# Two transformer layers on one core: the first five attention units of layer 2 take their keys in two parts

## The chip, the cores and the metric

The kernel runs on one core of a Trainium2 chip. Five engines work side by side and meet only through semaphores: TensorE (PE, matrix products into PSUM), VectorE (DVE), ScalarE (ACT), GpSimd (POOL) and SyncE (SP, which here issues the DMAs). The metric is the device time of one execution in microseconds (us). Before the change the median of three runs is 2412.53 us (2412.13 to 2412.62).

## The reference

Two layers, each an attention block and a gated feed-forward block, both with a layer norm ahead and a residual around them. The sequence has 2048 tokens of width 512, the attention 32 heads of 16, the feed-forward a width of 1792. Both layers use the same weights.

```python
def _A_ref(x, wqkv, wo):
    ...
    scores = jnp.einsum("bhqd,bhkd->bhqk", q, k) * (Dh ** -0.5)
    p = _softmax(scores, axis=-1)
    o = jnp.einsum("bhqk,bhkd->bhqd", p, v)
    return (...o...) @ wo

def _B_ref(x, w_gate, w_up, w_down):
    return (_gelu(x @ w_gate) * (x @ w_up)) @ w_down

x = A_x
x = x + _A_ref(_layernorm(x), A_wqkv, A_wo)
x = x + _B_ref(_layernorm(x), B_w_gate, B_w_up, B_w_down)
x = x + _A_ref(_layernorm(x), A_wqkv, A_wo)
x = x + _B_ref(_layernorm(x), B_w_gate, B_w_up, B_w_down)
```

## The kernel before

Everything stays in on-chip memory. The attention is cut into **units**: four heads (a group `g`, of eight) times one block of queries (512, at the end of a layer less). A unit runs through two passes over all 2048 keys:

- **Pass 1** finds the maximum of each row of scores. PE multiplies 128 queries by 512 keys into one PSUM bank (L2935), DVE reduces the bank to one column of `PM` (L2950), one bank at a time ("128x1") or two banks in one instruction ("128x2"). A unit has 64 such tiles. Six small POOL operations (`fin_step`, from L1956) join the four key blocks' maxima into minus the row maximum, which is turned around (a DMA, or for the units at a layer's edge a DVE transpose into `MT`, L1972) and written by DMA into spare rows of the query tile `QT`.
- **Pass 2** multiplies in the other direction, keys by queries (L2813). The spare rows make the product come out as score minus maximum. ACT takes the exponential into one of ten slots `PT` of the buffer `SCR` (L2785), again one bank (512 columns) or two (1024) in one instruction. PE multiplies that by the values `VP`, which carry a column of ones for the row sums, and sums over all keys in PSUM bank 7 (L2838). At a unit's end `nrm` copies bank 7 to `ACCS` (ACT, L2034), and POOL divides by the row sums into `ATT`.

A **fold** takes work from DVE to ACT: PE multiplies the queries by the difference of two key blocks (`KD`), ACT writes its positive part to a slot (Relu, L2765), and one DVE instruction (L2945) adds that to the other block's scores and takes the maximum, in place of two reductions.

Beside the two passes run the projections, the output product, the layer norms and the feed-forward. Their PSUM banks are emptied by ACT or DVE. `evac` (L1592 for DVE, L1594 for ACT) and `x_add` (L2053 for DVE, L2058 for ACT) decide this by how far pass 1 is ahead of pass 2. The keys of a layer-2 block need the finished tokens of layer 1, so the keys 1536 to 2047 of layer 2 come only after the last feed-forward block of layer 1. The last block's gate uses the Gelu table of ACT, during which no exponential of pass 2 is emitted (`gel["on"]`).

The order of all instructions is made ahead of time, by a planner in the program (from L2980 on): it keeps a clock for each engine with estimated durations and emits, at each step, a pass-1 tile, a pass-2 tile or a piece of other work. A table `PLAN` gives it 20 parameters for every two pairs of pass-1 tiles (priorities, lags between the passes, how many banks each pass may take). The chip then runs the order as it stands.

At the edge between the layers the planner has this: pass 1 of the first six units of layer 2 (`n_pre=6`) does its first three key blocks as soon as these keys exist, 48 tiles for each unit, and its fourth block later. Pass 2 of a unit begins when the maximum over all four blocks is in `QT`, thus after the last keys of layer 2.

Of the kernel before, what the change touches and what calls it, by code (L numbers as in the profile page):

```python
# [12 lines left out]
AP = bass.AP  # L13

DH = 16
# [8 lines left out]
    1: (0.1, 0.0, 0.65, 0.52, 0.2, -0.3, 2, 0, 22, 16, 8, 20, 0.7, 4.0, -20, 10, 2, 2, 11, 84),  # L24
    2: (0.3, 0.25, 0.8, 0.42, 0.2, 0.0, 1, 1, 30, 92, 3, 80, 0.5, 2.5, 10, 18, 2, 1, 7, 30),
    3: (0.3, 0.5, 0.55, 0.42, 0.0, 0.0, 3, 1, 62, 92, 3, 80, 0.4, 0.5, -5, 18, 2, 4, 3, 68),
    4: (0.15, 0.25, 0.25, 0.42, 0.0, -0.2, 2, 1, 70, 160, 8, 80, 0.5, 3.0, -5, 18, 2, 3, 7, 60),
    5: (0.3, 0.25, 0.65, 0.42, 0.1, -0.05, 3, 1, 14, 92, 8, 60, 0.5, 2.5, 0, -6, 3, 3, 7, 16),
    6: (0.2, 0.0, 0.55, 0.52, 0.2, -0.05, 2, 2, 14, 44, 8, 60, 0.7, 4.0, 0, -6, 2, 1, 7, 100),
    7: (0.1, 0.05, 0.65, 0.52, 0.2, -0.05, 2, 2, 46, 160, -10, 60, 1.0, 1.5, 20, -14, 2, 2, 7, 84),  # L30
    9: (0.1, 0.05, 0.65, 0.52, 0.2, -0.05, 2, 2, 46, 160, -10, 60, 1.0, 2.5, 20, -14, 3, 2, 7, 84),
    10: (0.3, 0.05, 0.65, 0.52, 0.2, -0.05, 2, 2, 62, 68, 8, 100, 1.0, 2.0, 20, 2, 2, 2, 11, 84),
    11: (0.3, 0.25, 0.65, 0.22, 0.0, -0.05, 2, 1, 110, 124, 8, 80, 0.3, 2.5, 0, 10, 1, 3, 3, 124),
    12: (0.3, 0.25, 0.25, 0.62, 0.0, -0.05, 2, 1, 110, 124, 8, 80, 0.3, 1.0, 0, 10, 1, 3, 3, 68),
    13: (0.3, 0.25, 0.55, 0.42, 0.7, 0.0, 2, 1, 62, 92, 3, 80, 0.4, 1.5, 0, 18, 2, 1, 8, 100),
    15: (0.0, 0.05, 0.65, 0.52, 0.2, -0.05, 2, 2, 62, 68, 8, 100, 1.0, 2.0, 20, 2, 2, 2, 11, 84),
    16: (0.3, 0.35, 0.55, 0.52, 0.0, 0.0, 3, 2, 110, 100, 3, 40, 0.4, 4.0, -10, 18, 1, 4, 6, 44),
    17: (0.3, 0.25, 0.55, 0.42, 0.7, 0.0, 2, 1, 62, 92, 3, 80, 0.4, 1.5, 0, 18, 2, 1, 8, 100),
    18: (0.3, 0.35, 0.55, 0.52, 0.0, 0.0, 3, 2, 110, 100, 3, 40, 0.4, 4.0, -10, -14, 1, 4, 14, 92),
    19: (0.3, 0.05, 0.65, 0.52, 0.2, -0.05, 2, 2, 62, 68, 8, 40, 1.0, 2.0, 20, 2, 2, 2, 11, 84),  # L40
    22: (0.3, 0.25, 0.45, 0.42, 0.7, 0.0, 3, 1, 62, 92, 3, 80, 0.4, 4.0, -5, 18, 4, 1, 3, 30),
    23: (0.3, 0.05, 0.55, 0.42, 0.0, 0.0, 3, 1, 62, 92, 3, 80, 0.4, 0.5, -5, 18, 2, 4, 3, 68),
    24: (0.3, 0.05, 0.55, 0.42, 0.0, 0.0, 3, 1, 62, 92, -10, 80, 0.4, 0.5, -5, 18, 2, 4, 3, 68),
    25: (0.3, 0.05, 0.65, 0.22, 0.0, 0.0, 2, 1, 110, 124, 13, 80, 0.3, 2.5, 0, 10, 1, 3, 3, 124),
    26: (0.3, 0.25, 0.25, 0.12, 0.3, 0.0, 3, 1, 62, 92, 3, 60, 0.4, 4.0, -5, 18, 2, 1, 8, 68),
    27: (0.3, 0.25, 0.55, 0.42, 0.7, 0.0, 3, 2, 62, 92, 13, 100, 0.5, 4.0, -5, -6, 1, 3, 7, 68),
    28: (0.3, 0.25, 0.55, 0.42, 0.7, 0.0, 3, 2, 62, 92, 8, 100, 0.5, 4.0, -5, 2, 1, 3, 7, 68),
# [12 lines left out]
    41: (0.2, 0.25, 0.65, 0.62, 0.0, -0.05, 2, 0, 0, 84, 13, 40, 0.0, 0.5, -20, -14, 2, 3, 8, 92),  # L60
    43: (0.3, 0.5, 0.55, 0.52, 0.3, -0.05, 2, 0, 22, 84, 8, 20, 0.3, 2.0, 10, -14, 2, 2, 7, 84),
    45: (0.3, 0.5, 0.55, 0.52, 0.3, -0.05, 2, 0, 22, 84, 13, 20, 0.3, 2.0, 10, -14, 2, 2, 7, 84),
    47: (0.3, 0.15, 0.55, 0.82, 0.5, -0.05, 2, 2, 22, 16, 8, 60, 1.0, 0.5, -10, 10, 2, 3, 6, 84),
    48: (0.3, 0.15, 0.35, 0.32, 0.5, -0.05, 2, 2, 22, 16, 8, 60, 1.0, 0.5, 5, 10, 2, 3, 6, 84),
    49: (0.3, 0.35, 0.65, 0.82, 0.7, -0.05, 2, 0, 22, 100, 13, 40, 0.3, 2.5, -10, -14, 4, 2, 3, 0),
    50: (0.2, 0.25, 0.45, 0.62, 0.2, -0.2, 2, 2, 30, 84, 8, 60, 0.7, 4.0, 0, -6, 1, 1, 8, 100),
    51: (0.2, 0.25, 0.8, 0.62, 0.2, -0.2, 2, 2, 30, 84, 13, 60, 0.7, 4.0, 0, -6, 1, 1, 8, 100),
    52: (0.2, 0.25, 0.65, 0.62, 0.2, -0.2, 2, 2, 30, 84, 8, 60, 0.7, 4.0, 0, -6, 1, 1, 8, 100),
    53: (0.2, 0.0, 0.55, 0.32, 0.5, -0.1, 2, 0, 38, 84, 3, 100, 0.1, 2.0, 0, 6, 1, 1, 7, 60),
    54: (0.15, 0.5, 0.55, 0.82, 0.3, -0.05, 3, 2, 22, 30, 8, 60, 0.7, 2.5, 0, -14, 2, 4, 3, 100),  # L70
    55: (0.3, 0.25, 0.55, 0.42, 0.1, -0.05, 2, 1, 14, 92, 8, 60, 0.5, 2.0, 0, 18, 3, 3, 7, 44),
# [24 lines left out]
    85: (0.1, 0.35, 0.65, 0.62, 0.2, -0.3, 2, 0, 22, 16, 8, 20, 0.7, 4.0, -20, -6, 2, 3, 7, 84),
# [3109 lines left out]
```

## Time and profile before

| | |
|---|---|
| median of 3 runs | 2412.53 us |
| the profiled execution's own time | 2412.13 us |
| its span, first to last instruction | 2410.4 us |
| TensorE clock granted, mean | 0.999 |
| busy: PE, DVE, ACT, POOL | 2352.4, 2360.6, 2313.4, 1344.2 us |
| pass 1: reductions of one bank, of two | 1436, 1109 |
| pass 2: exponentials of one bank, of two | 1044, 1526 |

An execution's own time is 1.7 us longer than its span. Busy time counts an instruction from its start to its end, and what two instructions of one engine share is counted once. Fillers: the 1724 matmuls of L2968 multiply zeros to keep PE occupied, so PE's busy share says little of its real load.

### The profile page before, as it was taken

How to read it: one execution, taken by the hardware profiler on the slowest of the kernel's cores; microseconds unless marked ns; L12 is line 12 of the kernel's file. 1: busy time of each engine (PE TensorE's matmuls, PEld its weight loads, DVE VectorE, ACT ScalarE, POOL GpSimd, SP SyncE). 2: the span in 40 equal slices, each digit the busy share in tenths (PEclk: the TensorE clock that was granted, in tenths of full speed). 3: DMA queues.
4: the chain of work that ended last, by engine and by line, in shares of the span. 5: the costliest groups of instructions: out<-in, count | busy, mean ns of one | idle time of the engine just before them, and what ended most of it. 6: DMA issues, size and time to landing. Idle time of an engine off the chain costs nothing.

```text
span 2410.4 us, 69140 instructions
## 1 busy us (share of the span) xinstructions
PE 2352.4 (98%) x29692; PEld 1136.4 (47%) x29692; DVE 2360.6 (98%) x3191; ACT 2313.4 (96%) x3252; POOL 1344.2 (56%) x2239
## 2 busy tenths in 40 slices
PE   9999999999999999999999999999999999999999
PEld 4444444444444444444534555544444444444456
DVE  9999999999999999999999999999999999999994
ACT  7999999999999999999975999999999999999996
POOL 5121147967779575977742221178717882379452
PEclk9999999999999999999999999999999999999999
DMA  3110000000000001001010000000000000000000
GB/s 97 50 62 10 3 16 14 3 5 9 21 12 3 5 13 21 8 5 26 17 25 15 7 5 5 14 14 2 5 12 21 8 3 10 16 15 5 14 13 13
DMA packets 77166, 37.50 MB, mean 16 GB/s; under 512 B 59068, under 2 KB 75836, under 8 KB 76860
## 3 DMA queue, kind: packets, MB, share of 16 engines
q1 hardware_dynamic: 76860, 33.10, 5.7%
q8 instruction: 232, 3.80, 0.6%
q14 instruction: 74, 0.61, 0.1%
HBM read 9.70 MB, written 2.10 MB: 5 GB/s over the span
## 4 chain that ended last, share of the span: by engine, by line
DVE 51%; PE 32%; ACT 16%; issue 1%; POOL 0%; POOLq 0%; DVEq 0%; ACTq 0%
DVE PM L2950 46%; ACT SCR L2785 14%; PE PS L2935 11%; PE PS L1577 9%; PE PS L2838 8%; PE PS L2813 3%; DVE SCR L2945 2%; PE PS L2968 1%; ACT SCR L2765 1%; DVE HT L1375 0%; DVE ST L1629 0%; ACT SCR L2197 0%; PE PS L2758 0%; ACT HT L1594 0%; ACT SG L1594 0%
## 5 line engine op out<-in xcount | busy, mean ns | idle before, releaser
L2950 DVE TENSOR_REDUCE PM<-PS 128x1 f32<-128x512 f32 (+1 forms) x2545 | 2152.4, 916 | 9.2 <-PE PS L2935 2.5
L2785 ACT ACTIVATE SCR<-PS 128x1024 bf16<-128x1024 f32 (+1 forms) x2570 | 2012.6, 898 | 25.5 <-PE PS L2813 15.7
L2935 PE MATMUL PS<-KT,QT 32*128 32x512 bf16 x3875 | 1045.7, 385 | 41.3 <-DVE PM L2950 24.6
L2813 PE MATMUL PS<-QT,KT 32*128 32x512 bf16 (+2 forms) x5120 | 931.0, 340 | 2.2 <-ACT SCR L2765 0.8
L2838 PE MATMUL PS<-VP,SCR 128*128 128x51 bf16 (+1 forms) x16384 | 817.7, 188 | 3.7 <-ACT SCR L2785 1.8
L2838 PEld LDWEIGHTS PS<-VP,SCR 128*128 128x128 bf16 x16384 | 578.3, 96 | 502.9 <-issue 445.6
L2935 PEld LDWEIGHTS PS<-KT,QT 32*128 32x128 bf16 x3875 | 249.2, 91 | 501.3 <-DVE PM L2950 311.5
L2040 POOL TENSOR_TENSOR RL<-ACCS,CM 128x16 f32<-128x16 f32 (+2 forms) x70 | 181.1, 2587 | 310.9 <-ACT ACCS L2034 310.3
L2968 PE MATMUL PS<-WV,CON 128*128 128x240 bf16 x1724 | 320.4, 266 | 0.4 <-ACT SCR L2785 0.4
L2813 PEld LDWEIGHTS PS<-QT,KT 32*128 32x128 bf16 x5120 | 241.4, 91 | 61.8 <-ACT SCR L2785 34.1
L1956 POOL TENSOR_TENSOR PM<-PM 128x32 f32<-128x32 f32 (+2 forms) x80 | 19.1, 239 | 329.1 <-DVE PM L2950 317.4
L2968 PEld LDWEIGHTS PS<-WV,CON 128*128 128x128 bf16 x1724 | 132.6, 96 | 42.3 <-issue 36.7
L2945 DVE CUSTOM_DVE_ANT_0 SCR<-PS,SCR 128x512 bf16<-128x512 f32 x221 | 141.0, 685 | 1.3 <-PE PS L2813 0.8
L1577 PE MATMUL PS<-WD,HT 128*128 128x512 bf16 x448 | 140.6, 381 | 0.0
L1577 PE MATMUL PS<-XNT,WU 128*128 128x512 bf16 (+2 forms) x616 | 136.3, 323 | 0.1
L1577 PE MATMUL PS<-XNT,WG 128*128 128x512 bf16 (+2 forms) x616 | 135.4, 323 | 0.5 <-ACT XNT L1594 0.5
L2453 POOL TENSOR_TENSOR HT<-HT,AO 128x512 bf16<-128x512 bf16 (+1 forms) x91 | 98.6, 1086 | 52.0 <-ACT AO L2451 50.8
L2765 ACT ACTIVATE SCR<-PS 128x1024 bf16<-128x1024 f32 (+1 forms) x112 | 117.5, 1059 | 8.8 <-PE PS L2758 6.5
L2191 POOL TENSOR_TENSOR SCR<-HT 128x512 bf16<-128x512 bf16 x98 | 101.8, 1039 | 32.8 <-ACT HT L1594 26.3
L2513 POOL TENSOR_TENSOR KD<-KT 128x512 bf16<-128x512 bf16 x78 | 89.9, 1153 | 48.4 <-PE PS L2758 46.7
L2201 POOL TENSOR_TENSOR HT<-HT,SCR 128x512 bf16<-128x512 bf16 x98 | 112.9, 1152 | 3.6
L2195 POOL TENSOR_TENSOR SCR<-SCR,HT 128x512 bf16<-128x512 bf16 x98 | 112.8, 1152 | 1.9
(130 smaller groups left out, 1490.0 us busy)
## 6 DMA issues: line engine op xcount, KB each, us to landing
KT<-SG SPq DMA_DIRECT2D x64, 64.0 KB
QT<-SG SPq DMA_DIRECT2D x52, 64.0 KB
out_dram<-AO SPq DMA_DIRECT2D x16, 128.0 KB, 1.7
WG<-in_B_w_gate_dram SPq DMA_DIRECT2D x4, 448.0 KB, 5.0
WU<-in_B_w_up_dram SPq DMA_DIRECT2D x4, 448.0 KB, 4.8
WD<-in_B_w_down_dram SPq DMA_DIRECT2D x4, 384.0 KB, 3.7
PM<-CON SPq DMA_TRANSPOSE x70, 2.2
HT<-in_A_x_dram SPq DMA_DIRECT2D x2, 512.0 KB, 9.1
```

The costliest lines, as they stand in the source:

```text
L1577: ins = e.matmul(out_ap, lhsT=l, rhs=r_, start=(i == 0), stop=(i == n - 1))
L2040: emit("pool", lambda e: e.tensor_tensor(RL[:, s, 0:4 * nq], lsum, CM1[:, 0:4 * nq], op=ALU.pow), r=[("ACCS", s), ("CM1",)], w=[("RL", s)] ...
L2195: emit("pool", lambda e: e.tensor_tensor(u, u, ht, op=ALU.mult), r=ku + kh, w=ku, dur=0.18 + n / 520.0)
L2201: emit("pool", lambda e: e.tensor_tensor(ht, ht, u, op=ALU.mult), r=ku + kh, w=kh, dur=0.18 + n / 520.0)
L2765: emit("act", lambda e: e.activation(PT[:, s0:s0 + cnt, :], PS[:, bk:bk + cnt, :], ACTF.Relu), r=bks, w=[("PT", s0 + d) for d in range(cnt ...
L2785: emit("act", lambda e: e.activation(dst, src, ACTF.Exp, scale=DH ** -0.5), r=[BK[bk + i] for i in range(cnt)], w=[("PT", i) for i in slot ...
L2813: ins = e.matmul(bank(bk)[:, i * n:(i + 1) * n], lhsT=KT[32 * j:32 * j + 32, g, kt * 128:(kt + 1) * 128], rhs=QT[32 * j:32 * j + 32, s, c0 ...
L2838: ins = e.matmul(acc, lhsT=PT[:, slot, i * nh + (qt - q0) * 128:i * nh + (qt - q0 + 1) * 128], rhs=AP(VP, (kt * H + 4 * g + j) * 17, [[NTT ...
L2935: ins = e.matmul(bank(b), lhsT=QT[32 * j:32 * j + 32, s, qt * 128:(qt + 1) * 128], rhs=KT[32 * j:32 * j + 32, g, kb * 512:(kb + 1) * 512], ...
L2945: emit("dve", lambda e, i=i, b=b, sl=sl: e.tensor_tensor_reduce(PT[:, sl, :], bank(b), PT[:, sl, :], 1.0, -3.0e38, ALU.add, ALU.max, po[:, ...
L2950: emit("dve", lambda e: e.tensor_reduce(po, PS[:, bs[0]:bs[0] + cnt, :], axis=AX.X, op=ALU.max), r=bks, w=[("PM", sm) + h[1:] for h in hs] ...
L2968: return e.matmul(PS[:, b, NACC:512], lhsT=ZER, rhs=ZR[:, 0, 0:512 - NACC], start=(b != 7), stop=(b != 7), skip_group_check=True)
```

## The change

The first five units of layer 2 (`u_two`, all of 512 queries) do both passes in two parts.

- **Part 0**: after the first three key blocks (48 tiles) POOL makes the maximum over these 1536 keys (seven small operations), a DVE transpose and four DMAs write it into `QT`, and pass 2 runs over the first 12 of 16 key tiles of each head. The unit's sums then go from bank 7 to `ACCS` (ACT) and by POOL to a parking place: one of the ten `PT` slots as 32-bit numbers, the row sums to `SC`.
- **Part 1**: pass 1 of the fourth key block runs with the first maximum already in `QT`, so its result is the excess over that maximum. POOL makes the new maximum from it and the difference of the two; a transpose and four DMAs write it; pass 2 runs over the last four key tiles. A small exponential on ACT (`two_f`) gives the factor, POOL rescales the parked sums, and at the end adds them to those of part 1 and divides.
- Pass 2 takes the ten jobs in the order part 0 of five units, then part 1 of the five units.
- The values of layer 2 are projected in chunks of four token tiles by two head groups (`VCH=1`), with earlier due times where part 0 needs them.
- The layer norm on POOL that uses `SC` doesn't start while two-part units are in pass 2 or parked.
- `PLAN` has 879 entries instead of 895, and nearly all of them have other numbers.

```diff
-VCH=0, ... MQD=0.4):
+VCH=1, ... MQD=0.4, NPA=5, PAV=24):
...
+            u0 = min(u for u in range(NU) if units[u][0] == la)
+            if NPA:
+                u_two = list(range(u0, u0 + NPA))
...
-        def qh_count(u, qt):
+        def qh_count(u, qt, kb):
+            if u in u_two:
+                p = 0 if kb < NKB - 1 else 1
+                two_left[u, p] -= 1
+                if not two_left[u, p]:
+                    fin_wait.append({"u": u, "stage": 0, "h": 0, "part": p})
+                return
...
-                yield ("cond", lambda tt=tt, i=i: ready(tt) and at["tr"] > i - 2)
+                yield ("cond", lambda tt=tt, i=i: ready(tt) and at["tr"] > i - 2 and not two_busy())
...
+                else:
+                    k = pk[0] + pk[1] + pk[3]
+                    sf = ("SCF", u_two.index(u))
+                    fa = SC[:, 16 * u_two.index(u):16 * u_two.index(u) + 16].rearrange("p (a k) -> p a k", a=nq)
+                    emit("pool", lambda e: e.tensor_scalar(c1, c3, 0.0, None, op0=ALU.max), r=k, w=k, dur=d)
+                    emit("pool", lambda e: e.tensor_tensor(mo, c0, c1, op=ALU.subtract), r=k, w=[("MSEL", u % 2)], dur=d)
+                    emit("pool", lambda e: e.tensor_tensor(fa, mo, c0, op=ALU.subtract), r=[("MSEL", u % 2)] + k, w=k + [sf], dur=d)
...
         def f_dma(u):
-            return DM and qh[u] == 1 and u + DMX[units[u][0]] <= u_end[units[u][0]]
+            return DM and qh[u] == 1 and u not in u_two and u + DMX[units[u][0]] <= u_end[units[u][0]]
...
+        def two_f(u):
+            i = u_two.index(u)
+            fa = SC[:, 16 * i:16 * i + 16]
+            emit("act", lambda e: e.activation(fa, fa, ACTF.Exp, scale=DH ** -0.5), r=[("SCF", i)], w=[("SCF", i)], dur=0.08)
...
+            emit("pool", lambda e: e.tensor_tensor(av, av, fb, op=ALU.mult), r=[("SCF", i), ("PT", sl)], w=[("PT", sl)], dur=0.6)
+            emit("pool", lambda e: e.tensor_tensor(la_, la_, fa, op=ALU.mult), r=[("SCF", i)] + two_key(i), w=two_key(i), dur=0.2)
...
-        def nrm(u):
+        def nrm(u, part=None):
...
+            if part == 0:
+                i = u_two.index(u)
+                sl = slot_one()
+                pt_busy[sl] = -2
+                two_acc[u] = sl
+                two_live.add(u)
+                emit("act", lambda e: e.activation(ACCS[:, s, 0:na], PS[:, 7, 0:na], ACTF.Copy),
+                     r=[BK[7]], w=[("ACCS", s)], dur=0.05 + na / 1200.0)
+                ...
+                return
...
-                    add(vproj_c(la, c, b), last_p1[u0 + 2 * c] + VD + 8 * b)
+                    add(vproj_c(la, c, b), first_p1[u0] - PAV + 4 * b + 24 * c if la and b < NKB - 1 and 2 * c < NPA else last_p1[u0 + 2 * c] + VD + 8 * b)
...
-        p2 = {"u": 0, "h": 0, "todo": None}
+        jobs = [(u, None) for u in range(NU) if u not in u_two]
+        jobs[u_two[0] if u_two else 0:0] = [(u, p) for p in range(2) for u in u_two]
+        p2 = {"i": 0, "u": 0, "h": 0, "todo": None, "part": None}
...
+            if u in u_two and kb == NKB - 1 and not qh_done[u]:
+                return None
```

What the planner makes of it can be read from the order of each engine's instructions. Three places matter below. The rows give the line in the file, the operation, what it writes and reads, and its count.

The first is ACT at the edge between the layers, around the table load for the last Gelu of layer 1 (`VP` are values of layer 2, `SG` staged keys, `HT` the feed-forward's hidden block, `AO` its staging buffer). Before:

```order
L1594 ACTIVATE SG<-PS 128x512
L1594 ACTIVATE VP<-PS 128x32x16
L2765 ACTIVATE SCR<-PS 128x1024
L1594 ACTIVATE VP<-PS 128x32x16
L2765 ACTIVATE SCR<-PS 128x1024
L1594 ACTIVATE VP<-PS 128x32x16 x4
L2413 ACT_TABLE_LOAD
```

And now, where L2863 is the exponential of pass 2 and L2486 the Gelu:

```order
L2863 ACTIVATE SCR<-PS 128x512
L1598 ACTIVATE VP<-PS 128x4x8x16
L2863 ACTIVATE SCR<-PS 128x1024
L2863 ACTIVATE SCR<-PS 128x512
L2863 ACTIVATE SCR<-PS 128x1024
L1598 ACTIVATE VP<-PS 128x4x8x16 x2
L2486 ACT_TABLE_LOAD
L2486 ACTIVATE HT<-PS 128x256 x14
L2863 ACT_TABLE_LOAD
L2863 ACTIVATE SCR<-PS 128x512
```

Exponentials of layer 2 stand ahead of the Gelu and directly behind it, where only copies and the Relu of folds (L2765) stood. The second table load, which stood behind the last keys of layer 2, has come to the end of the Gelus.

The second place is DVE where the last keys of layer 2 are copied out of PSUM (`SG`), the end of what pass 1 can do without them. Before:

```order
L2950 TENSOR_REDUCE PM<-PS 128x2
L2950 TENSOR_REDUCE PM<-PS 128x1
L1592 CAST SG<-PS 128x512
L2950 TENSOR_REDUCE PM<-PS 128x2 x6
L1972 STREAM_TRANSPOSE MT<-CON 128x32
```

And now:

```order
L3035 TENSOR_REDUCE PM<-PS 128x1
L3035 TENSOR_REDUCE PM<-PS 128x2
L1596 CAST SG<-PS 128x512 x2
L3035 TENSOR_REDUCE PM<-PS 128x2
L3035 TENSOR_REDUCE PM<-PS 128x1 x3
```

In both, DVE's reductions of the first three key blocks end just ahead of these copies. Between the last exponential of layer 1 and this place stood 30 Relu instructions of folds and 137 pass-1 tiles that PE and DVE read plainly or folded; now no fold stands there, 195 pass-1 tiles do, and on ACT 104 exponentials of one bank and 40 of two, together 184 tiles.

The third place is DVE in the first feed-forward block of layer 2, after some 2680 pass-1 tiles of 3875. Before:

```order
L2950 TENSOR_REDUCE PM<-PS 128x1 x7
L1592 CAST HT<-PS 128x512
L2950 TENSOR_REDUCE PM<-PS 128x1 x3
L1592 CAST HT<-PS 128x512
L2950 TENSOR_REDUCE PM<-PS 128x1 x5
L1592 CAST HT<-PS 128x512
L2950 TENSOR_REDUCE PM<-PS 128x1 x6
```

And now, at the same count of tiles:

```order
L3035 TENSOR_REDUCE PM<-PS 128x2
L3035 TENSOR_REDUCE PM<-PS 128x1
L3035 TENSOR_REDUCE PM<-PS 128x2
L3035 TENSOR_REDUCE PM<-PS 128x1
L3035 TENSOR_REDUCE PM<-PS 128x2
```

The copies of the hidden block are gone from DVE there, and its reductions read two banks in every second instruction.

117 lines of the change are left out of this document (90 added, 27 removed), and 1764 rows, old and new, of the table PLAN.

## Prediction

> **What bounds the kernel now.** I read the page's busy times and slices first, then the busy times by stage, then DVE's instructions by form.
>
> ```profile
> PE 2352.4 (98%) x29692; PEld 1136.4 (47%) x29692; DVE 2360.6 (98%) x3191; ACT 2313.4 (96%) x3252; POOL 1344.2 (56%) x2239
> DVE  9999999999999999999999999999999999999994
> ACT  7999999999999999999975999999999999999996
> DVE 51%; PE 32%; ACT 16%; issue 1%; POOL 0%; POOLq 0%; DVEq 0%; ACTq 0%
> ```
>
> DVE is busy for 2360.6 of 2410.4 us, with a gap only in the last slice, and it holds half of the chain that ended last. So the time is DVE's sum plus its few gaps. ACT, with 2313.4 us, has gaps in the first slice, in the last, and in slices 20 and 21: the edge between the layers.
>
> ```profile
> 1206.00:1300.00 94.00, 89.66 (x549) 35.76 (x547) 90.94 (x184) 60.42 (x93) 39.25 (x85) 1.00 0.13 25
> 1300.00:1545.00 245.00, 238.74 (x3353) 124.35 (x3351) 244.75 (x300) 235.69 (x261) 47.99 (x91) 1.00 0.02 5
> 1545.00:1741.00 196.00, 193.41 (x2443) 90.82 (x2439) 195.02 (x274) 195.44 (x240) 144.15 (x217) 1.00 0.04 10
> 2361.00:2410.00 49.00, 44.32 (x666) 30.47 (x664) 15.53 (x49) 29.27 (x57) 7.73 (x15) 1.00 0.05 15
> ```
>
> The columns after the length are the busy times of PE, its weight loads, DVE, ACT and POOL, then PE's granted clock. From 1206 to 1300 us ACT has 60.4 us of work in 94: idle 33.6. From 1300 to 1545 it is idle 9.3 more. DVE is nearly full in both, so filling ACT gives nothing there by itself; ACT must take something off DVE. From 1545 to 1741 both are full.
>
> ```profile
> 1244.67 0.60 ACT L1594 ACTIVATE VP<-PS 128x512 bf16<-128x512 f32 x1 [1.11 <-PE PS L1577]
> 1245.29 1.28 ACT L2413 ACT_TABLE_LOAD   x1
> ...
> 1297.81 1.28 ACT L2785 ACT_TABLE_LOAD   x1
> 1308.18 1.94 ACT L2785 ACTIVATE SCR<-PS 128x1024 bf16<-128x1024 f32 x2 [9.09 <-PE PS L2813]
> ```
>
> ACT's first exponential of layer 2 starts at 1308.18, after a wait of 9.09 us for the last keys and the maximum. From then on pass 2 is behind, and the planner's rule for emptying banks (`evac`, `x_add`) sends copies to DVE while pass 1 leads by much. That is seen in DVE's forms from 1545 to 1741 us, the first feed-forward block of layer 2:
>
> ```profile
> L2950 DVE TENSOR_REDUCE PM<-PS 128x1 f32<-128x512 f32 x201 | 129.7, 685 | 0.9 <-PE PS L2813 0.3
> L2950 DVE TENSOR_REDUCE PM<-PS 128x2 f32<-128x1024 f32 x51 | 62.1, 1218 | 0.0
> L1592 DVE CAST HT<-PS 128x512 bf16<-128x512 f32 x12 | 8.2, 683 | 0.1
> ...
> L2950 DVE TENSOR_REDUCE PM<-PS 128x2 f32<-128x1024 f32 x98 | 119.5, 1219 | 0.1
> L2950 DVE TENSOR_REDUCE PM<-PS 128x1 f32<-128x512 f32 x135 | 89.4, 682 | 0.0
> ```
>
> The last two rows are the stretch ahead, 1350 to 1545. There 331 tiles (2 x 98 + 135) pass in 195 us, 0.589 us each. From 1545 to 1741 only 303 pass in 196 us, since DVE also copies and reads bank by bank.
>
> **The change, part by part.** The order of the changed kernel is fixed, so DVE's instructions can be counted in it and priced with rows of the whole trace, busy time over count:
>
> ```profile
> L2950 DVE TENSOR_REDUCE PM<-PS 128x2 f32<-128x1024 f32 x1109 | 1348.1, 1218 | 6.0 <-PE PS L2935 2.2 <-PE PS L2813 0.9
> L2950 DVE TENSOR_REDUCE PM<-PS 128x1 f32<-128x512 f32 x1436 | 958.7, 682 | 3.1 <-PE PS L2935 0.3 <-PE PS L2813 0.3 <-PE PS L2758 0.2
> L1592 DVE CAST HT<-PS 128x512 bf16<-128x512 f32 x16 | 10.9, 682 | 0.1
> L1972 DVE STREAM_TRANSPOSE MT<-CON 128x32 bf16<-128x32 bf16 x10 | 2.0, 204 | 1.7 <-POOL CON L1961 1.7
> ```
>
> 1. *Reductions.* The tiles read stay 3875 and the folds 221. Two-bank reads go from 1109 to 1164, one-bank reads from 1436 to 1326. At 1348.1/1109 = 1.216 and 958.7/1436 = 0.668 us that is 55 x 1.216 - 110 x 0.668 = 66.9 - 73.5 = **-6.6**. At worst it is nothing, if DVE then waits for PE instead.
> 2. *Copies and additions that go from DVE to ACT.* Casts of the hidden block 16 to 8, casts of staged keys and queries 8 to 2 (one of these of half width), additions to `X` 6 to 2, products of the feed-forward (L2428, L2445 in full width) 13 to 12, and two of half width new. That is 18 fewer of full width, at 10.9/16 = 0.68 us -12.2, and one half-width operation more, +0.4: **-11.8**.
> 3. *Transposes.* 10 to 18, at 0.20 us: **+1.6**. The ten waited 1.7 us for POOL, so eight more may wait **+1.4**.
>
> Together -6.6 - 11.8 + 1.6 + 1.4 = **-15.4 us**. The stage agrees: 303 tiles at the rate of the stretch ahead take 303 x 0.589 = 178 us instead of 196, 18 less, and nearly all of the removed copies are in that stage. Bounds of these terms: -8.8 if the reductions give nothing, -18.
>
> 4. *The last keys.* DVE still runs out of work where they come. Before:
>
> ```profile
> 1290.77 2.41 DVE L2950 TENSOR_REDUCE PM<-PS 128x1 f32<-128x512 f32 x3
> 1293.99 0.69 DVE L1592 CAST SG<-PS 128x512 bf16<-128x512 f32 x1 [0.81 <-PE PS L1577]
> 1296.22 6.88 DVE L2950 TENSOR_REDUCE PM<-PS 128x2 f32<-128x1024 f32 x6 [1.53 <-PE PS L2935]
> ```
>
> Waits of 0.81 and 1.53, together 2.3 us. In the new order the copies of the last keys again stand behind the last tile that needs no last keys, so this wait stays; it can go, -2.3, or grow, because on the way to these keys (output product, layer norms, last feed-forward block, Gelu, keys) ACT and PE now have exponentials to do between. DVE has more to do meanwhile too: 195 tiles at 0.589 are 115 us, with six layer-norm statistics and the other small work some 121. For ACT, two rows give the price, and a third what of the old 60.4 us was folds, which are gone:
>
> ```profile
> L2785 ACT ACTIVATE SCR<-PS 128x1024 bf16<-128x1024 f32 x1526 | 1470.8, 1081 | 21.3 <-PE PS L2813 14.0
> L2785 ACT ACTIVATE SCR<-PS 128x512 bf16<-128x512 f32 x1044 | 595.1, 631 | 4.2 <-PE PS L2813 1.8
> ...
> L2765 ACT ACTIVATE SCR<-PS 128x1024 bf16<-128x1024 f32 x30 | 30.7, 1023 | 7.9 <-PE PS L2758 5.9 <-PE PS L2935 1.5
> ```
>
> 104 exponentials of one bank at 595.1/1044 = 0.570 and 40 of two at 0.964 are 98 us; with 60.4 - 30.7 = 30 us of the old work and a table load, 129. Against DVE's 121 that would make the keys 8 us late; the 0.570 holds waiting for PE, though, so I take the row of before once more, **+2.3**, and keep -2.3 and +8 for the range.
>
> 5. *Parking and merging.* Five copies of bank 7, five factor exponentials, on ACT; sixteen small POOL operations a unit in place of six; two lots of four DMAs a unit on SP. POOL is at 56% and the page's chain has 0% of it; SP has no other long queue there than the staged keys, which stand behind the part-0 maxima of all five units in its order. Queued behind a late maximum on SP would be those keys, so this cost is in the range of term 4. A transpose on DVE that waits holds the reductions behind it and so PE's banks: that is in term 3. I put the rest at **0**; without the cover of ACT's idle 43 us the copies would cost 5 x 0.45 us.
>
> 6. *The end.* From 2361 us DVE has 15.5 us of work in 49; the order there is nearly the same, with 42 tiles of pass 2 left behind the last reduction instead of 44. **0**.
>
> Sum: -15.4 + 2.3 = -13.1 on the profiled execution's 2412.1 (span 2410.4 and 1.7 around it, 0.4 below the median): **2399 us**.
>
> **The rivals.** *ACT becomes the bound.* ACT's one-bank exponentials go from 1044 to 1394, the two-bank ones from 1526 to 1351: 350 x 0.570 - 175 x 0.964 = +30.8 us. The 18 operations come over at about 0.63 (+11), parking and factors add 4: 46 in all. ACT would have 2359 us of work, and its idle time outside the edge, 97.0 - 42.9 = 54, would put the end at 2413 + 1.7 = 2415. For it: this sum is as good as DVE's. Against it: the order has 150 of the 350 in the 320 tiles soon after layer 1, where ACT was idle, and a one-bank exponential is taken where ACT has time. At nothing for the splitting it ends at 2384, below DVE's bound; so in between, 2400 to 2415, near 2407. The Trainium skill, "ScalarE: Activation LUTs", section "What ACT_TABLE_LOAD costs", speaks against splitting: it gives an activation a fixed 186 ns, of which 93 overlap with the next, so 175 splits would be, as an estimate, 16 us, and this rival's end 2400. The trace agrees with a fixed part (631 ns for 512, 1081 for 1024, so 181 left over); no run here shows what of it overlaps.
>
> *The keys come late* (slower). If the waits on the way to the last keys can't be used for exponentials, ACT's 33.6 us of idle time in that stretch come on top of 129: 163 against DVE's 121, and DVE stands for 42 us instead of 2. That is 2439. It decides from 18 us of standing on, where the gain is eaten (2414), and shows as slower from 23. Against it: all waits of the old stretch had idle ACT around them, and the layer-1 stages run such a feed-forward beside exponentials with DVE full.
>
> *The early exponentials don't come early.* Then time stays at 2412. The order shows them ahead of the Gelu's table load, so only a wait on the maxima could do it. I give this nothing of its own.
>
> *More than the sum.* With the copies gone and pass 2 less behind, the small gaps of the stages behind 1545 may shrink too: 18 and 5 less, 2389.
>
> **How the numbers follow.** The forecast (2392 to 2404) has 0.63, ACT as the bound 0.21, late keys past 23 us 0.06, more than the sum 0.10. A change of 0.2%, 4.8 us, is about what can be told from none. Faster by more than that, below 2407.7: 0.63 + 0.10 and half of 0.21, 0.83. Within it: the other half, 0.11. Slower: 0.06. The range goes from 2389 to 2411: it takes in the bounds of terms 1 to 4 (-18 - 2.3 on one side, -8.8 + 8 on the other), and leaves out the worst of ACT's case and the late keys.
>
> **What would show it.** Term 2: DVE's cast and addition rows from 1545 on nearly empty, and 303 tiles there in about 180 us. Term 4: the wait ahead of the first reduction behind the copies of the last keys, 2 to 4 us; over 10 and the slower rival is on. The rival of ACT: idle time of DVE that waits for pass 2 through PE, and one-bank exponentials back to back at over 0.55 us. The forecast is wrong if DVE's busy time doesn't fall by about 15 us, or falls and gaps take its place.

## The result and the profile after

The changed kernel takes 2398.97 us (median of 4 runs, 2398.49 to 2399.44), the kernel before in the same session 2412.57 (4 runs, 2412.13 to 2415.3). The ratio is 0.9941, with a 95% interval of 0.9924 to 0.9958. The prediction was 2399.0.

The page of the changed kernel, the lines that answer to those of before (busy time by engine, the slices of DVE and ACT, the chain that ended last):

```profile
PE 2344.3 (98%) x29728; PEld 1139.1 (48%) x29728; DVE 2345.9 (98%) x3127; ACT 2332.7 (97%) x3455; POOL 1366.4 (57%) x2287
...
DVE  9999999999999999999999999999999999999994
ACT  7999999999999999999998999999999999999986
...
DVE 51%; PE 36%; ACT 12%; issue 1%; POOL 0%; DMA 0%; SPq 0%; POOLq 0%; ACTq 0%; DVEq 0%
```

DVE has 2360.6 - 2345.9 = 14.7 us less to do, and ACT 2332.7 - 2313.4 = 19.3 more. ACT's hole in slices 20 and 21, counted from 0 (7 and 5 before), is all but closed (9 and 8). DVE's idle time in the span went from 2410.4 - 2360.6 = 49.8 to 2396.8 - 2345.9 = 50.9 us, so the span's 13.6 us are 14.7 of busy time less 1.1 of new waiting.

The same stretches of time (columns as before: length, busy times of PE, its weight loads, DVE, ACT, POOL, then PE's clock):

```profile
1206.00:1300.00 94.00, 92.65 (x1090) 45.42 (x1087) 93.41 (x114) 87.86 (x156) 39.75 (x72) 1.00 0.10 20
1300.00:1545.00 245.00, 239.39 (x3106) 119.28 (x3103) 239.48 (x326) 242.44 (x334) 82.93 (x159) 1.00 0.05 10
1545.00:1741.00 196.00, 193.17 (x2330) 88.15 (x2330) 195.46 (x248) 194.22 (x299) 135.77 (x204) 1.00 0.04 8
```

At the edge ACT now has 87.9 us of work in 94, where it had 60.4. What it does there, in its timeline (start, length, the instruction; in brackets the idle time before it):

```profile
1224.98 3.18 ACT L2863 ACTIVATE SCR<-PS 128x1024 bf16<-128x1024 f32 x5
1228.33 7.85 ACT L2863 ACTIVATE SCR<-PS 128x1024 bf16<-128x1024 f32 x13 [0.16 <-PE PS L2895]
...
1236.62 3.26 ACT L2863 ACTIVATE SCR<-PS 128x512 bf16<-128x512 f32 x6
```

These are exponentials of layer 2, some 80 us ahead of the first one of before (1308.18). Counted by PSUM banks, 2048 to a layer, the first of layer 2 starts at 1210.5, 98 us earlier than before. Where that time is paid back is seen on PE from 1545 to 1741 us. The two lines with `KT,QT` and `QT,KT` are the tiles of pass 1 and of pass 2. Before:

```profile
L2935 PE MATMUL PS<-KT,QT 32*128 32x512 bf16 x302 | 95.5, 385 | 1.9 <-DVE PM L2950 1.2 <-DVE HT L2445 0.2
L2813 PE MATMUL PS<-QT,KT 32*128 32x512 bf16 x387 | 80.3, 385 | 0.3
```

And after, with DVE's instructions of the same stretch:

```profile
L3020 PE MATMUL PS<-KT,QT 32*128 32x512 bf16 x332 | 87.7, 384 | 1.9 <-DVE PM L3035 0.4 <-ACT SCR L2863 0.3
L2895 PE MATMUL PS<-QT,KT 32*128 32x512 bf16 x345 | 85.8, 384 | 0.1
```

```profile
L3035 DVE TENSOR_REDUCE PM<-PS 128x2 f32<-128x1024 f32 x103 | 124.8, 1218 | 0.3 <-PE PS L2895 0.2
L3035 DVE TENSOR_REDUCE PM<-PS 128x1 f32<-128x512 f32 x112 | 75.5, 682 | 0.2
...
L1596 DVE CAST HT<-PS 128x512 bf16<-128x512 f32 x1 | 0.7, 681 | 0.0
```

In the same 196 us PE feeds 30 more tiles of pass 1 and 42 fewer of pass 2. ACT, with fewer exponentials to do, takes the copies, and DVE is left with one cast of the twelve.

The times at which DVE had read the n-th of the 3875 tiles of pass 1, worked out from both traces, show where the gain is made:

| tiles read | before, us | after, us | difference |
|---|---|---|---|
| 1800 (layer 1) | 1090.4 | 1094.4 | +4.0 |
| 2150 (edge) | 1309.3 | 1305.0 | -4.3 |
| 2250 (behind the last keys) | 1367.3 | 1371.7 | +4.4 |
| 2550 | 1544.8 | 1549.9 | +5.1 |
| 2850 (end of the first feed-forward block) | 1739.8 | 1727.2 | -12.6 |
| 3750 | 2280.3 | 2264.3 | -16.0 |
| 3875 (all) | 2360.8 | 2348.1 | -12.7 |

Up to tile 2550 nothing is won. Between 2550 and 2850 it is 17.7 us. The new order gives back 4 us in layer 1 and 3 in the last 125 tiles.

How far pass 2 has come by then, counted the same way, as banks of exponentials of layer 2 that ACT has done:

| tiles read | before | after | head start |
|---|---|---|---|
| 2129 (the last keys of before) | 0 | 117 | 117 |
| 2250 | 124 | 259 | 135 |
| 2550 | 506 | 594 | 88 |
| 2850 | 890 | 903 | 13 |
| 3750 | 1877 | 1874 | -3 |

The edge gives pass 2 a head start of some 135 banks. 88 are left at tile 2550, and 75 of them are used up by tile 2850: beside the same 300 tiles of pass 1 ACT does 309 banks where it did 384. This is the stretch in which the time is won, and in it all three engines have less to do. From tile 2550 to tile 2850, before and after:

```profile
1544.79:1739.83 195.04, 192.45 (x2439) 90.58 (x2438) 194.06 (x274) 194.48 (x239) 144.15 (x217) 1.00 0.04 10
1549.87:1727.22 177.35, 174.64 (x2102) 79.47 (x2100) 176.87 (x222) 175.88 (x272) 129.14 (x192) 1.00 0.03 8
```

PE has 17.8 us less of busy time, DVE 17.2 and ACT 18.6, and each is nearly full in both. (The ends of PE's matmuls are modelled in the profile, so its busy time tells the direction here, not how near PE is to a limit.)

### The profile page after: what moved, and what is told of

Read it like the earlier page. It is cut to its first block, busy times and chain, and to the rows that moved or that the text cites. A ratio compares the mean times of both kernels' runs of the same rounds, so it can differ in the third digit from the quotient of the medians.

```text
span 2396.8 us, 69428 instructions
## 1 busy us (share of the span) xinstructions
PE 2344.3 (98%) x29728; PEld 1139.1 (48%) x29728; DVE 2345.9 (98%) x3127; ACT 2332.7 (97%) x3455; POOL 1366.4 (57%) x2287
## 4 chain that ended last, share of the span: by engine, by line
DVE 51%; PE 36%; ACT 12%; issue 1%; POOL 0%; DMA 0%; SPq 0%; POOLq 0%; ACTq 0%; DVEq 0%
DVE PM L3035 47%; PE PS L3020 12%; ACT SCR L2863 10%; PE PS L2920 9%; PE PS L1581 9%; PE PS L2895 4%; DVE SCR L3030 3%; PE PS L3053 2%; ACT SCR L2841 1%; PE PS L1909 0%; ACT SCR L2270 0%; ACT AO L2524 0%; PE PS L2834 0%; ACT SG L1598 0%; DVE ST L1636 0%
## 5 line engine op out<-in xcount | busy, mean ns | idle before, releaser
L2863 ACT ACTIVATE SCR<-PS 128x512 bf16<-128x512 f32 (+1 forms) x2745 | 2039.5, 848 | 21.2 <-PE PS L2895 8.6
L2895 PE MATMUL PS<-QT,KT 32*128 32x512 bf16 (+2 forms) x5056 | 964.9, 342 | 3.6 <-ACT SCR L2863 2.4
L3053 PE MATMUL PS<-WV,CON 128*128 128x240 bf16 x1632 | 300.8, 266 | 0.6 <-ACT SCR L2863 0.3
L2895 PEld LDWEIGHTS PS<-QT,KT 32*128 32x128 bf16 x5056 | 249.6, 91 | 71.3 <-ACT SCR L2863 39.8
L1987 POOL TENSOR_TENSOR PM<-PM 128x32 f32<-128x32 f32 (+2 forms) x74 | 17.8, 240 | 272.0 <-DVE PM L3035 259.9
L1581 PE MATMUL PS<-WD,HT 128*128 128x512 bf16 x448 | 146.2, 380 | 0.0
L3053 PEld LDWEIGHTS PS<-WV,CON 128*128 128x128 bf16 x1632 | 124.3, 96 | 38.2 <-issue 32.8
L2841 ACT ACTIVATE SCR<-PS 128x1024 bf16<-128x1024 f32 (+1 forms) x113 | 119.2, 1065 | 0.3
```

The lines of the kernel that those rows point to most:

```text
L1581: ins = e.matmul(out_ap, lhsT=l, rhs=r_, start=(i == 0), stop=(i == n - 1))
L2841: emit("act", lambda e: e.activation(PT[:, s0:s0 + cnt, :], PS[:, bk:bk + cnt, :], ACTF.Relu), r=bks, w=[("PT", s0 + d) for d in range(cnt ...
L2863: emit("act", lambda e: e.activation(dst, src, ACTF.Exp, scale=DH ** -0.5), r=[BK[bk + i] for i in range(cnt)], w=[("PT", i) for i in slot ...
L2895: ins = e.matmul(bank(bk)[:, i * n:(i + 1) * n], lhsT=KT[32 * j:32 * j + 32, g, kt * 128:(kt + 1) * 128], rhs=QT[32 * j:32 * j + 32, s, c0 ...
L3053: return e.matmul(PS[:, b, NACC:512], lhsT=ZER, rhs=ZR[:, 0, 0:512 - NACC], start=(b != 7), stop=(b != 7), skip_group_check=True)
```

## The experiments

The forecast held that DVE's sum of work is the time. Its first rival held that ACT becomes the bound. The experiments add work to one engine, take work off one engine, or move it, and leave the order of everything else as the planner made it (its clocks don't see the edits). In eight of their traces some 250 of the 29,700 matmuls have no record (those of all runs below but b_dve18, b_near, b_near_nofill and a_dve7_keys), so PE's busy time reads low there and isn't used. "Before" was run beside each group: 2412.61, 2412.45, 2412.47 and 2412.36 us. Kernels made from the changed one are also set against its 2398.97 of another session. The diffs are cut to the lines that matter; `n_read` counts the tiles read.

### Work added to the changed kernel: DVE, then ACT

```diff
+if tile_in(2540, 2870) and cnt_x[1] < 20:     # every 10th one, 20 in all
+    sch.op("dve", lambda e: e.tensor_reduce(SQ[:, 1, 0:1], bank(bs[0]), axis=AX.X, op=ALU.max), ...)
 emit("dve", lambda e: e.tensor_reduce(po, PS[:, bs[0]:bs[0] + cnt, :], ...
```

> The changed kernel, with 20 more one-bank reductions on DVE in the first feed-forward block of layer 2 (tiles 2540 to 2870 of pass 1), each of a bank that DVE reads anyway, into a column that nobody reads. The order of everything else is the same. A reduction in a run of its kind starts 0.60 us after the one before it. DVE as the bound: 20 x 0.60 = +12.0, 2411. ACT as the bound there: DVE has time to spare, under +3, 2399 to 2402.

```diff
+    sch.op("act", lambda e: e.activation(PT[:, free[0], :], bank(bk), ACTF.Exp, scale=DH ** -0.5), ...)
 emit("act", lambda e: e.activation(dst, src, ACTF.Exp, scale=DH ** -0.5), ...
```

> The changed kernel, with 20 more one-bank exponentials on ACT in the same stretch, each of a bank that ACT reads anyway, into a free slot. Back to back a one-bank exponential takes 0.48 us. DVE alone as the bound: ACT is a little behind for a while and makes it up, 0 to +3, 2399 to 2402. ACT as the bound, alone or together with DVE: 20 x 0.48 = +9.6, 2408.6. Both this run and the one with reductions at full price would mean that the two engines are full together, and neither alone is the bound.

Measured: 2410.49 us with the reductions (11 runs, 2409.53 to 2413.25; ratio to before 0.9992, interval 0.9983 to 1.0), +11.5. And 2408.56 with the exponentials (11 runs, 2407.51 to 2411.89; 0.9985, 0.9976 to 0.9994), +9.6. Each is the full price or nearly: 11.5 of 12.0, and 9.6 of 9.6. The block from 1545 to 1741, first with the reductions, then with the exponentials:

```profile
1545.00:1741.00 196.00, 178.58 (x2173) 82.27 (x2198) 195.64 (x251) 186.86 (x282) 134.69 (x203) 1.00 0.03 8
```

```profile
1545.00:1741.00 196.00, 187.11 (x2160) 85.46 (x2184) 186.45 (x231) 191.83 (x298) 135.29 (x203) 0.97 0.03 8
```

With more work on DVE, ACT falls from 194.2 to 186.9 us of work and waits. With more on ACT, DVE falls from 195.5 to 186.5 and waits. This profiled execution also lost some of PE's clock there, 0.97, and lies at the upper end of its runs: 4.0 of DVE's 9.5 idle us are in the 24 us around that loss, 5.5 are not. So neither engine alone is the bound of this stage. Work added to either one lengthens it, and both the forecast's picture and the rival's are half of it.

### Work added at the edge, before and after

The extra reading stands ahead of each of 19 folds (before, Relu) or of every fourth exponential (after, 19 in all), written as above.

> The kernel before, with 19 more one-bank readings on ACT at the edge between the layers (ahead of 19 folds, tiles 1985 to 2140), into a free slot. ACT has 43 us without work there. Idle time that costs nothing: 0 to +2, 2412 to 2414. If ACT is on the way to the last keys there in spite of its gaps: up to 19 x 0.48 = +9.1, 2421.

> The changed kernel, with 19 more one-bank exponentials on ACT in the same tiles of pass 1, 1985 to 2140, each of a bank that it reads anyway, into a free slot. If the early exponentials have used up the idle time of ACT and ACT's work after it counts: +9.1, 2408. If DVE alone is the bound: 0 to +3, 2399 to 2402.

Measured: before with the edit 2419.18 us (9 runs, 2418.47 to 2423.06; 1.0025, 1.0016 to 1.0035), +6.6. After with the edit 2407.79 (11 runs, 2407.4 to 2411.64; 0.9981, 0.9972 to 0.999), +8.8.

The second is as expected for a used-up gap, 8.8 of 9.1. The first is not: 43 us of idle ACT, and 19 short instructions in it still cost 6.6 of 9.1. The edge of that kernel:

```profile
1206.00:1300.00 94.00, 84.73 (x504) 33.35 (x509) 87.25 (x178) 66.11 (x107) 39.19 (x84) 1.00 0.11 19
```

ACT is idle for 28 of 94 us there, and DVE now too for 6.7 where it was 3.1. An instruction ahead of a fold holds the fold's PSUM bank longer; PE's next tiles wait for it, and DVE waits for PE. The trace bears this out: in this stretch PE waits 4.5 us for the folds' Relu, which it didn't wait for before, and DVE waits 5.3 us for PE's tiles (2.0 before). Idle time on an engine is thus no free place: it depends on what stands behind the added instruction in the order.

### The copies alone, room on ACT alone, and both

```diff
-    emit("dve", lambda e: e.tensor_copy(dst, src), ...
+    sch.op("act", lambda e: e.activation(dst, src, ACTF.Copy), r=r, w=w)      # b_casts_act, tiles 2540 to 2860
...
+    if cnt == 2 and tile_in(2540, 2860) and ...:                              # b_less_exp: every fifth, 25 in all
+        src, dst = src[:, :, 0:16], dst[:, :, 0:16]
     emit("act", lambda e: e.activation(dst, src, ACTF.Exp, scale=DH ** -0.5),
```

The four additions to `X` among the 18 operations become a copy on ACT and an addition on POOL (not shown in the diff). The shortened exponentials leave out the rest of their results.

> The kernel before, without parts and with its own order; only the 18 operations that DVE does beside its reductions in the first feed-forward block of layer 2 (12 casts of the hidden block, 2 of staged queries, 4 additions to X) are done by ACT, as the kernel does them elsewhere. DVE has 18 x 0.66 = 12 us less, ACT 18 x 0.49 = 9 more. If where these operations run were all of the gain: -12, 2400. My theory, by which ACT must have room for them first: no gain, 0 to +9, 2412 to 2421.

> The kernel before, with room made on ACT only: 25 two-bank exponentials of tiles 2540 to 2860 compute 16 columns of each bank in place of 512 (the rest of their results is left out), 25 x 0.85 = 21 us less on ACT. Nothing is taken off DVE. DVE as the bound: 0 to -4, 2408 to 2412. ACT as the bound there: -10 to -21, 2391 to 2402.

> The two edits on the kernel before together: room on ACT (the same 25 exponentials shortened, the rest of their results left out) and the 18 operations moved from DVE to ACT. My theory: the gain of the change comes back without its parts, 18 x 0.66 = -12 less small waits, 2400 to 2403. If the gain of the change lies in its new order of work and not in the copies, little: 2408 to 2412.

Measured: copies alone 2420.46 us (6 runs, 2419.99 to 2420.85; 1.0033, 1.002 to 1.0045), +8.0. Room alone 2412.10 (11 runs, 2411.52 to 2414.85; 1.0001, 0.9992 to 1.001), -0.4. Both 2420.74 (5 runs, 2418.05 to 2421.78; 1.0033, 1.002 to 1.0045), +8.3.

The first two are as the theory had it: the copies alone cost 8.0 us, since ACT is full there (195.6 of 196 us in that run's block); room alone gives nothing. The third is not. My theory said 2400 to 2403. From 1545 to 1741 us of b_both:

```profile
1545.00:1741.00 196.00, 184.71 (x2333) 88.02 (x2357) 179.45 (x246) 180.26 (x246) 145.58 (x218) 0.98 0.04 9
```

DVE stands for 196 - 179.5 = 16.5 us and ACT for 15.7, nearly all of it waiting for PE. Half of the loss is one event: PE waits 1.81 us for a normalised block (`XNT`, at 1628.70), its clock falls behind it, and between tiles 2680 and 2700 this run goes from +1.1 to +5.2 us against before. The same event is met again in b_near below. The rest comes bit by bit up to tile 2780, as in the run with the copies alone. So b_both doesn't show the two reliefs by themselves; without the event some 4 us of loss would be left, and no gain.

The reverse, on the changed kernel:

> The changed kernel, with its order; 16 copies of the first feed-forward block of layer 2 (13 casts of the hidden block, 3 of staged keys and queries) are taken back from ACT to DVE. DVE has 16 x 0.66 = 10.6 us more, ACT 16 x 0.48 = 7.7 less. DVE as the bound: +10.6, 2409.6. ACT as the bound there: -7.7 to 0, 2391 to 2399.

Measured: 2407.97 us (11 runs, 2406.36 to 2410.6; 0.9983, 0.9974 to 0.9991), +9.0 of 10.6. The copies taken back to DVE cost nearly their full price, and ACT's relief of 7.7 us gives nothing. Any other work added to DVE there would cost the same (a_dve20 above), so this doesn't say that the gain was made by moving them.

### Work taken off DVE alone, and room at the place

```diff
+if tile_in(2540, 2860) and not fast:                                          # b_dve18; x_add likewise
+    dst, src = dst[..., 0:16], src[..., 0:16]
 emit("dve", lambda e: e.tensor_copy(dst, src), ...
```

> The kernel before, with its order. The same 18 operations of the first feed-forward block of layer 2 stay on DVE but compute 16 columns of 512 (the rest of their results is left out): some 0.1 us each in place of 0.66, 18 x 0.55 = 10 us less on DVE. ACT has the work that it had. DVE as the bound by itself: -10, 2402. DVE and ACT locked together by PE's fixed order, with ACT full in that stretch: relief of DVE alone gives nothing, 0 to -2, 2410 to 2412.

> The kernel before, with its order, the 18 operations on ACT as in b_casts_act, and room made for them at the place: the two-bank exponential ahead of each of them and the one behind it compute 16 columns of each bank (the rest of their results is left out), 36 x 0.85 = 31 us less on ACT, 9 more for the copies. If the room has to be where the copies are (PE holds both engines in step within a few banks): DVE's 18 x 0.66 = 12 us come back, all or half of them, 2400 to 2406, where b_both, with the room elsewhere in the same stretch, gave +8.3. If it isn't the place but the fixed order as a whole that keeps the gain from showing: 2412 to 2420.

Measured: b_dve18 2412.38 us (11 runs, 2411.72 to 2415.16; 0.9999, 0.999 to 1.0008), -0.1. Ten microseconds less work on the engine that is 98% busy, and no gain. Its block, in which ACT is as full as before, and what is left of the casts there:

```profile
1545.00:1741.00 196.00, 193.51 (x2454) 91.30 (x2451) 188.43 (x274) 195.44 (x240) 144.21 (x217) 1.00 0.04 10
```

```profile
L2959 DVE TENSOR_REDUCE PM<-PS 128x1 f32<-128x512 f32 x200 | 130.5, 686 | 6.3 <-PE PS L2822 3.8 <-PE PS L2944 1.4
...
L1600 DVE CAST HT<-PS 128x16 bf16<-128x16 f32 x12 | 2.0, 166 | 0.1
```

The casts take 2.0 us where they took 8.2, and the next reductions wait 6.3 us for PE where they waited 0.9 (the row of before in the prediction).

b_near, with room on ACT beside every copy: 2416.86 us (11 runs, 2414.5 to 2420.66; 1.0019, 1.001 to 1.0028), +4.4. By the tile count as in the table above it is at -0.4 against before at tile 2650 and at +3.7 at 2700, and stays there. The event between is one wait of PE for a normalised block, in its timeline, and the two windows of 20 us around it:

```profile
1627.23 0.59 PE L1578 MATMUL PS<-XNT,WG 128*128 128x512 bf16 x2 [1.79 <-DMA XNT<-XN]
```

```profile
1605.00:1625.00 20.00, 18.82 (x267) 9.07 (x265) 19.51 (x24) 19.29 (x24) 17.30 (x40) 1.00 0.07 16
1625.00:1645.00 20.00, 18.21 (x196) 7.55 (x193) 13.96 (x22) 12.98 (x24) 11.20 (x16) 0.83 0.05 10
```

The additions to `X`, moved to ACT and POOL, come later that way, and so does the layer norm (this is argued from the order of the work; no run takes it apart). PE stands for 1.8 us, and its granted clock is 0.83 in the window of it: 20 x 0.17 = 3.4 us more, of which, with the wait, 4.1 reach the tile count. Outside of this event b_near gains nothing, though its whole block shows DVE with 195.0 - 183.0 = 12 us less work and ACT with 195.4 - 175.4 = 20 less:

```profile
1545.00:1741.00 196.00, 191.16 (x2396) 88.73 (x2392) 182.96 (x251) 175.43 (x253) 147.60 (x220) 0.98 0.04 10
```

So the place wasn't the answer either. In this block all that DVE and ACT wait for, 12.1 and 19.1 us, is PE, and PE is idle for 4.8 us, the event included. That points at PE's own stream.

### Is PE's own stream what holds both?

PE's stream has filler matmuls in it, at places where the planner saw PE idle. With the engines relieved they might be what is left.

```diff
-emit_pe(fn, 1, 512 - NACC, r=[("ZER",), (ZRK,)], w=[BK[b]])
+emit_pe(fn, 1, 512 - NACC, r=[("ZER",), (ZRK,)], w=[BK[b]], put=not tile_in(2540, 2860))
```

> b_near (both engines relieved in the first feed-forward block of layer 2; 15/16 or more of 36 exponentials left out) without the filler matmuls of that stretch (78 products with zeros, 0.26 us each, 67 of them and 17 us of PE's time between 1545 and 1741), which the order put where the planner saw PE idle. b_near gained nothing outside one wait of PE for a normalised block (1.8 us, and a clock of 0.83 in the 20 us around it, +4). If PE's own stream, full at 191 of 196 us with the fillers in it, is what holds both engines there: -8 to -12 against b_near, 2405 to 2409. If the waits from engine to engine in the fixed order hold them: 2415 to 2417, as b_near. If PE's clock needs the fillers: granted clock clearly under 1 in more than the one slice, and 2417 or more.

Measured: 2429.16 us (6 runs, 2421.61 to 2436.97; 1.0072, 1.0051 to 1.0093), 12.3 more than b_near. The six fall into two groups, three of 2421.6 to 2424.1 and three of 2434.2 to 2437.0, with the median between them; the profile is of the first group. The third case came. The block in windows (PE's clock is the number behind POOL's):

```profile
1545.00:1605.00 60.00, 57.71 (x722) 27.61 (x719) 54.99 (x73) 54.23 (x69) 39.14 (x75) 0.83 0.09 19
1605.00:1625.00 20.00, 19.52 (x205) 8.23 (x202) 16.43 (x21) 15.78 (x20) 16.34 (x37) 0.67 0.07 14
1625.00:1645.00 20.00, 20.00 (x236) 9.04 (x232) 16.97 (x24) 17.07 (x25) 8.70 (x17) 0.73 0.05 10
...
1685.00:1725.00 40.00, 39.41 (x429) 17.03 (x428) 35.72 (x51) 34.48 (x52) 34.02 (x37) 0.87 0.01 1
```

The clock falls in four of the seven windows that it was read in. So this run doesn't say whether PE's stream held b_near: what it freed, the clock took. It does say that the fillers pay for themselves: its fastest execution is slower than the slowest of b_near (2420.66).

### Work added ahead of the last keys

> The changed kernel, with 7 more one-bank reductions on DVE in the tiles ahead of the last keys of layer 2 (from tile 2150 on), each of a bank that DVE reads anyway, into a column that nobody reads: 7 x 0.60 = 4.2 us. DVE stands for 1.87 + 2.49 = 4.4 us behind these tiles, since ACT and PE bring the keys late. If that wait is on their side: it takes up what is added, 0 to +1, 2399 to 2400. If the wait hangs on DVE's own speed (its banks hold PE back, and PE the keys): +4.2, 2403.

Measured: 2403.28 us (5 runs, 2402.13 to 2404.89; 0.9962, 0.995 to 0.9974), +4.3 of 4.2. DVE around the wait, first the changed kernel, then with the edit:

```profile
1324.02 5.25 DVE L3035 TENSOR_REDUCE PM<-PS 128x1 f32<-128x512 f32 x6
1331.14 0.69 DVE L1596 CAST SG<-PS 128x512 bf16<-128x512 f32 x1 [1.87 <-PE PS L1581]
1334.33 0.69 DVE L1596 CAST SG<-PS 128x512 bf16<-128x512 f32 x1 [2.49 <-PE PS L1581]
```

```profile
1328.37 5.25 DVE L3046 TENSOR_REDUCE PM<-PS 128x1 f32<-128x512 f32 x6
1335.50 0.69 DVE L1602 CAST SG<-PS 128x512 bf16<-128x512 f32 x1 [1.88 <-PE PS L1582]
1338.68 0.69 DVE L1602 CAST SG<-PS 128x512 bf16<-128x512 f32 x1 [2.49 <-PE PS L1582]
```

The waits of 1.88 and 2.49 us are there again to a hundredth; the whole place came 4.4 us later. DVE's reductions release the banks that PE needs ahead of the keys: from 1300 to 1345 us PE now waits 3.4 us for them, where it didn't wait for them at all. So a wait of DVE for PE was not room in which DVE could do more. The rival, not the first reading, holds.

## Why the prediction was right, and where its reason was not

**The number.** 2399.0 predicted, 2398.97 measured. It was a count of DVE's instructions in the new order, and the time is that count plus DVE's idle time as an identity. Term by term:

- *Reductions*, -6.6 predicted. The busy time of their two rows went from 1348.1 + 958.7 = 2306.8 to:

```profile
L3035 DVE TENSOR_REDUCE PM<-PS 128x2 f32<-128x1024 f32 x1164 | 1413.9, 1218 | 5.7 <-PE PS L2895 1.7 <-PE PS L3020 0.6
L3035 DVE TENSOR_REDUCE PM<-PS 128x1 f32<-128x512 f32 x1326 | 892.3, 682 | 2.4 <-PE PS L3020 0.4
...
L1596 DVE CAST HT<-PS 128x512 bf16<-128x512 f32 x8 | 5.5, 681 | 0.0
...
L2003 DVE STREAM_TRANSPOSE MT<-CON 128x32 bf16<-128x32 bf16 x18 | 3.6, 202 | 0.7 <-POOL CON L1992 0.7
...
L1596 DVE CAST SG<-PS 128x512 bf16<-128x512 f32 x2 | 1.4, 692 | 4.4 <-PE PS L1581 4.4
```

  2306.2, so 0.6 less. That form of busy time counts the overlap of neighbours only within a run of one shape, and the new order mixes shapes more. DVE's whole sum, where each overlap is counted once, fell by 14.7 where the terms said 6.6 + 11.8 - 1.6 = 16.8. With the other terms as they are, this one was about 2 us too large.
- *Copies and additions*, -11.8. The counts are those of the order; the casts of `HT` went from 10.9 to 5.5 us, those of `SG` in full width from seven to two.
- *Transposes*, +1.6 and +1.4 of waiting. Busy 3.6 instead of 2.0 is right; the eighteen wait 0.7 us in all where the ten waited 1.7. So this waiting was forecast 2.4 too high, which about made up for the reductions. In all, DVE's work was forecast 2.1 too low (-16.8, and -14.7 came) and its waits 2.6 too high (3.7, and 1.1 came); that the sum is right to a tenth is luck, that it is right to a few microseconds is not.
- *The last keys*, +2.3. The wait went from 2.3 to 1.87 + 2.49 = 4.4, +2.0 (before 0.81 + 1.53 = 2.34).
- *Parking and merging*, 0. The chain of the page has POOL at 0% still, POOL at 57%. No run took it away.
- *The end*, 0. Behind the last reduction 48.7 us are left, 49.6 before.
- *The stage check*, 303 tiles in 178 us. Now 332 pass in 196, which is 0.590 each and 179 for 303.

**The reason.** What failed are two sentences of the prediction's first part, read as a cause: "the time is DVE's sum plus its few gaps", in the sense that less work on DVE is less time, and "ACT must take something off DVE" as the way to it. In the order as it stands, work added costs its price or most of it (11.5 of 12.0 on DVE, 9.6 of 9.6 on ACT, 6.6 of 9.1 even in ACT's idle stretch). Work taken off one engine gives nothing (b_dve18 -0.1, b_less_exp -0.4), and off both neither (b_near, b_both). I read this as DVE, ACT and PE held in step by the few PSUM banks between them; no run takes that apart. So taking the 18 copies off DVE was not enough by itself. What changed is the order. The early exponentials give pass 2 a head start, and in the block that is gained from, PE, ACT and DVE are all relieved at once, by 17.8, 18.6 and 17.2 us for the same 300 tiles. Every edit within the old order left PE its stream of 385 tiles of pass 2 there, where it now has 309. That filling ACT "gives nothing there by itself" held at the place (-4.3 us at tile 2150, gone again at 2250); its worth came from tile 2550 on. DVE's count foretold the time because the planner fills DVE in either order.

**The rivals.** ACT as the bound was forecast as a rival of DVE as the bound. They are not alternatives: ACT's price is full as well, but its work rose by 19.3 us and not by 46, and it found 33 us of its idle time (97.0 before, 2396.8 - 2332.7 = 64.1 after). The late keys did not come: DVE stands 4.4 us at the place, far from 18. The early exponentials came early. For the price of splitting, the traces show the overlap that the prediction left open: where exponentials follow each other without a wait, those of 512 columns start 0.477 us apart and those of 1024 0.903, so one split costs 2 x 0.477 - 0.903 = 0.05 us and 175 of them some 9, against 30.8 in that rival's sum. *More than the sum* was right about the stages behind the block (-12.6 at tile 2850, -16.0 at 3750) and was eaten at both ends.

**What stays open.** How much of the 13.6 us a new order would have given without the two parts was not tried: each table of parameters is made for its own program. That the head start of pass 2 is the cause is read from the two traces and from the failure of every edit within the old order; no run takes the head start away or gives it alone. The 4 us given back in layer 1 and the 3 at the end are seen, not explained. That PE's own stream held b_near is read from its waits; the run meant to test it lost its clock.

## What to carry to other kernels

When several engines are above 95% busy in a fixed order, test one of them by adding work and by taking work away: a price for the added work says that the engine is on the path, and only a gain from the removed work says that it is the bound. A change that moves work between such engines must come with a new order, and its time is then counted in that order; the same move within the old one can cost as much as it was to bring. A wait before an engine is room for that engine only if the work ahead of it doesn't release what the awaited one needs.

## What the runs showed of the hardware

- The granted clock of PE can fall with hardly a gap. One wait of 1.79 us (b_near) was followed by a window of 20 us at 0.83, and one of 1.81 us (b_both) likewise. Without the fillers, 0.26 us each, it fell to 0.67 to 0.87 in four windows, and the median rose by 12.3 us. In a_act20 it fell at 1558 us with no wait of PE over 0.3 us in the 20 us ahead. A wait of 1.49 us at 20.9 us was followed by a clock of 0.91 over 20 us in the kernel before and of 1.00 in b_near_nofill. What decides it these runs don't show.
- Filling an engine's idle stretch is not always free: 9.1 us put into 43 us of idle ACT cost 6.6.
- In this fixed order delays neither grew nor were made up. Each edit's difference in time, once its stretch was over, stayed within 0.3 us over the rest of pass 1, 1000 tiles and more (b_casts_act +8.4 at tile 2800 and +8.3 at 3875; a_act19_edge +9.1 at 2250, +9.2 at 3875).
